# Attention of the first 768 tokens in tiles of four 32-query groups, ahead of two chained MLPs

## Chip, core and metric

One core of a Trainium2 chip. The metric is the device time of one launch in microseconds; for the kernel before it is 935.74 us, the median of three runs.

## What is computed

Four batches of 576 tokens with 8 heads of 64 channels go through an attention that adds two parts, and the 2304 x 512 result goes through two MLPs. All is float32 at the interface.

```python
# q, k, v: (4, 8, 576, 64); factor = 4; scale = 1 / 8
q_d, k_d, v_d = (x.reshape(B, H, 144, 4, D).mean(axis=3) for x in (q, k, v))
out_up = np.repeat(sm_attn(q_d, k_d, v_d), 4, axis=2)      # coarse attention over 144 averaged rows
mask = np.abs(pos[:, None] - pos[None, :]) < 4              # a band of 7 keys
out_local = softmax(where(mask, scale * q @ k.T, -1e9)) @ v
x = (out_up + out_local) as (2304, 512)
x = (s * relu(x @ w_in) ** 2 + b) @ w_out                   # d_ff 2048
x = ((x @ w_a) * (x @ w_b)) @ w_out2                        # d_ff 1536
```

## The kernel before

The program is written as a list of tasks (`Program.add`: an engine, a duration, what it reads, the buffers it takes and gives back, a due time), and `Program.order` plans it when the program is built: at each step it takes the task that could start first by its own model of times, and of equal ones the one that is due first. Each engine then runs its instructions in that order, so constants of the planner (`T0`, `DUE_*`, the durations, the numbers of buffers in `RAMP_BUFS`) move instructions on every engine.

There are three stages.

The **ramp** does the attention of tokens 0 to 767. `down` (L558) does the coarse attention of one pair of heads of one batch: keys and queries are loaded (L278) and added in fours (`prep`, on DVE at L582 for batch 0, on GpSimd at L584 and L585 for batch 1), then scores (L620), maxima (L634), exponentials (L647), normalisation (L662), transposes (L671) and the value product (L691). For batch 0 the pooled values are loaded in two halves of 72 rows per pair and summed by a reduction (L603); for batch 1 GpSimd's queue adds them up by transfers (L551). `tile_job` (L729) does the band of 7 keys for a tile of 96 tokens, all 8 heads: mask matmul (L774) and scores (L780) over 102 keys, maxima (L802), eight exponentials with an accumulator each (L816), normalisation of 816 elements (L831), eight transposes (L839), their copies (L849), the value product (L857), the sum with the coarse part (L871), and the split of the result into a high and a low part (`split_x`, L497 on ACT, L501 on DVE). There are eight such tiles, and a tile's 102 value rows come in one transfer. Between them PE runs matmuls on zeros (L273), whose number is planned, to keep busy.

The **first MLP** goes over six blocks of 384 tokens and 16 slices of d_ff each. A slice has 12 first-layer matmuls (L1059 to L1061, four groups of three) and 12 second-layer ones (L1102 to L1104), relu, square and copy on ACT (L1076 to L1083), and a subtraction on DVE (L1087). Block 0 needs its 32 weight slices decoded while it runs: each takes three ACT passes (L342, L349, L378) and three DVE passes (L354, L362, L383). The attention of the other 1536 tokens is done meanwhile, in `unit` on DVE. The **second MLP** (L1347 and L1487 to L1489) follows.

On SP all loads stand in one planned order, and POOL has its own. The change touches the ramp's tiles, loads and constants, and the planner.

```python
ts = add("PE", 1.75, s_fn, ..., [wide, wide, E_SLOT[ph]], ...,
    after=[mm["dS", b, hp] for hp in range(HP)], lead=LEAD, share=0.55)
```

This line of `tile_job` shows a task: a tile's scores come behind the coarse scores of its batch.

## Time and profile before

| | |
|---|---|
| runs | 934.76, 935.74, 935.96 us |
| span of the profiled execution | 932.3 us (its own time isn't given; the runs are 2.5 to 3.7 longer) |
| PE busy | 913.2 us, 98% |
| DVE busy | 789.9 us, 85% |
| ACT busy | 497.4 us, 53% |
| GpSimd busy | 69.7 us, 7% |
| first MLP matmul (L1059) | starts at 59.2 us |
| DMA, 0 to 60 us | 11.92 MB, 199 GB/s |
| DMA, 60 to 100 us | 296 GB/s, busy share 0.91 |

The shares are means over stages that differ: PE's 98% is full for most of the span, and its idle time is in the first 150 us. A busy time counts the overlap of neighbours, so the time from one start to the next is a little shorter than a duration. In the stretches, PEclk is the granted TensorE clock as a share of its full 2.4 GHz.

### The profile page before, as it was taken

Reading aid. Unit: us, or ns where it says so; the run is one execution under the profiler, and the core shown is the slowest. Engines: PE = TensorE matmul, PEld = TensorE weight load, DVE = VectorE, ACT = ScalarE, POOL = GpSimd, SP = SyncE. Lnnn points to the kernel's source line nnn. Section 1 sums busy time; section 2 is a strip of 40 time slices with the busy share of each in tenths; the row PEclk is TensorE's granted clock in tenths of the full one; section 3 lists DMA queues with packets and bytes.
Section 4 is the critical chain, followed back from the end, with each engine's and each line's share of the span. In section 5 each row is a group of like instructions: output and inputs, shape, how many; then the busy total and the mean of one; then the engine's idle time right before and its main releaser. Section 6 shows DMA issues by size and latency. Waiting matters only on the chain.

```text
span 932.3 us, 14367 instructions
## 1 busy us (share of the span) xinstructions
PE 913.2 (98%) x5319; PEld 847.0 (91%) x5319; DVE 789.9 (85%) x1388; ACT 497.4 (53%) x1144; POOL 69.7 (7%) x70
## 2 busy tenths in 40 slices
PE   8988999999999999999999999999999999999997
PEld 4667989998999899999999999999999999999996
DVE  6988998999999999995977999879877778877753
ACT  4989995345445443535988555335433336433322
POOL 2241201021322200000000000000000000000000
PEclk9998999999999999999999999999999999999999
DMA  7869626224354332313477342012200010300001
GB/s 206 241 174 332 156 90 194 82 82 133 115 115 114 103 107 69 102 29 136 148 262 261 122 122 82 23 44 81 102 22 3 24 43 13 102 29 18 1 1 69
DMA packets 46864, 96.76 MB, mean 104 GB/s; under 512 B 6393, under 2 KB 21337, under 8 KB 46409
## 3 DMA queue, kind: packets, MB, share of 16 engines
q1 hardware_dynamic: 39160, 92.77, 31.0%
q0 software_dynamic: 7200, 2.67, 2.5%
q8 instruction: 42, 0.69, 0.3%
q10 hardware_dynamic: 432, 0.39, 0.1%
q14 instruction: 30, 0.24, 0.1%
HBM read 83.22 MB, written 12.58 MB: 103 GB/s over the span
## 4 chain that ended last, share of the span: by engine, by line
PE 84%; DVE 5%; ACT 4%; issue 3%; DMA 2%; POOL 1%; SPq 0%; ACTq 0%
PE ab L1347 28%; PE acc L1102 7%; PE acc L1103 6%; PE h L1059 6%; PE acc L1104 6%; PE h L1061 6%; PE h L1060 6%; PE acc L1488 5%; PE acc L1489 5%; PE acc L1487 5%; DVE pr L969 1%; DMA pv<-in_vd_dram 1%; ACT z L342 1%; DMA tq<-in_bmask_dram 1%; ACT w L378 1%
## 5 line engine op out<-in xcount | busy, mean ns | idle before, releaser
L1347 PE MATMUL ab<-xo,w 128*128 128x384 f32 x1376 | 273.7, 338 | 0.4 <-DVE u L1390 0.4
L1347 PEld LDWEIGHTS ab<-xo,w 128*128 128x128 f32 x1376 | 246.1, 188 | 16.3 <-DVE u L1390 0.7
L1102 PE MATMUL acc<-gh,w 128*128 128x384 f32 (+1 forms) x384 | 134.2, 350 | 4.0 <-ACT w L816 2.0
L1103 PE MATMUL acc<-gl,w 128*128 128x384 f32 x384 | 131.2, 342 | 0.0
L1059 PE MATMUL h<-xsh,w 128*128 128x384 f32 x384 | 131.1, 341 | 0.0
L1104 PE MATMUL acc<-gh,w 128*128 128x384 f32 (+1 forms) x384 | 130.5, 340 | 0.0
L1061 PE MATMUL h<-xsh,w 128*128 128x384 f32 x384 | 129.0, 336 | 0.0
L1060 PE MATMUL h<-xsl,w 128*128 128x384 f32 x384 | 129.0, 336 | 0.0
L1076 ACT ACTIVATE u<-h 128x384 f32<-128x384 f32 x96 | 47.1, 491 | 116.3 <-PE h L1061 114.9
L1463 ACT ACTIVATE gh<-u 128x384 fp32r<-128x384 f32 x69 | 36.2, 524 | 84.6 <-DVE u L1424 50.5
L1102 PEld LDWEIGHTS acc<-gh,w 128*128 128x128 f32 x384 | 73.0, 190 | 8.1 <-ACT w L816 2.6
L1059 PEld LDWEIGHTS h<-xsh,w 128*128 128x128 f32 x384 | 72.2, 188 | 2.4 <-issue 2.0
L1103 PEld LDWEIGHTS acc<-gl,w 128*128 128x128 f32 x384 | 73.1, 190 | 0.9 <-DVE gl L1087 0.9
L1104 PEld LDWEIGHTS acc<-gh,w 128*128 128x128 f32 x384 | 73.0, 190 | 0.0
L1060 PEld LDWEIGHTS h<-xsl,w 128*128 128x128 f32 x384 | 72.2, 188 | 0.0
L1061 PEld LDWEIGHTS h<-xsh,w 128*128 128x128 f32 x384 | 72.1, 188 | 0.0
L1087 DVE TENSOR_TENSOR gl<-u,gh 128x384 fp32r<-128x384 f32 x96 | 54.3, 565 | 15.4 <-ACT gh L1083 15.2
L1371 ACT ACTIVATE w<-ab 128x384 f32<-128x384 f32 x31 | 15.2, 491 | 95.2 <-PE ab L1347 93.4
L1489 PE MATMUL acc<-w,gl 128*128 128x512 f32 x138 | 54.4, 394 | 0.0
L1488 PE MATMUL acc<-w,gh 128*128 128x512 f32 x138 | 54.3, 394 | 0.0
L1487 PE MATMUL acc<-w,gh 128*128 128x512 f32 x138 | 54.2, 393 | 0.0
L354 DVE TENSOR_SCALAR w<-w 128x512 uint16<-128x512 f32 x61 | 45.6, 767 | 8.3 <-ACT w L349 8.0
(207 smaller groups left out, 1743.9 us busy)
## 6 DMA issues: line engine op xcount, KB each, us to landing
w<-in_w_a_dram SPq DMA_DIRECT2D x26, 512.0 KB
w<-in_w_o_dram SPq DMA_DIRECT2D x25, 512.0 KB
bk<-in_ku_dram SPq DMA_DIRECT2D x22, 320.0 KB
bk<-in_vu_dram SPq DMA_DIRECT2D x22, 320.0 KB
w<-wod SPq DMA_DIRECT2D x12, 512.0 KB
w<-in_w_b_dram SPq DMA_DIRECT2D x10, 512.0 KB
x2d<-ev SPq DMA_DIRECT2D x24, 192.0 KB
x<-x2d SPq DMA_DIRECT2D x3, 1536.0 KB
```

The source lines that it names most:

```text
L1059: nc.tensor.matmul(out=st["h"], lhsT=w[:, 0, k], rhs=hi[:, k], start=(k == 0), stop=False)
L1060: nc.tensor.matmul(out=st["h"], lhsT=w[:, 0, k], rhs=lo[:, k], start=False, stop=False)
L1061: nc.tensor.matmul(out=st["h"], lhsT=w[:, 1, k], rhs=hi[:, k], start=False, stop=(k == HP - 1))
L1076: A_.activation(out=st["u"], in_=st["h"], func=ACTF.Relu)
L1087: V.tensor_tensor(out=st["lo"], in0=st["u"], in1=st["hi"][:, :n].bitcast(F32), op=ALU.subtract)
L1102: nc.tensor.matmul(out=acc, lhsT=wh, rhs=st["hi"], start=(f == 0), stop=False)
L1103: nc.tensor.matmul(out=acc[:, :n], lhsT=wh, rhs=st["lo"], start=False, stop=False)
L1104: nc.tensor.matmul(out=acc, lhsT=wl, rhs=st["hi"], start=False, stop=(f == FA - 1))
L1347: nc.tensor.matmul(out=o, lhsT=w[:, k], rhs=x, start=(not more and k + n == 0), stop=(k == 1 and n == 2), skip_group_check=more,)
L1487: nc.tensor.matmul(out=acc, lhsT=gh, rhs=w[:, 0], start=first, stop=False)
L1488: nc.tensor.matmul(out=acc, lhsT=gh, rhs=w[:, 1], start=False, stop=False)
L1489: nc.tensor.matmul(out=acc, lhsT=gl, rhs=w[:, 0], start=False, stop=last)
```

## The change

The ramp's 768 tokens are cut into six tiles of 128, and a tile into four groups of 32 queries, each with its own 38 keys. Scores of the four groups stand below one another in 128 partitions, so everything per tile runs over 8 x 38 = 304 elements in place of 816. The subtraction of the maximum is an instruction of its own on DVE (L872), the exponential is one ACT instruction (L882) with the sum as a DVE reduction (L888), and four transposes of 128 x 128 (L905) replace eight. In turn a tile has more matmuls: 32 for a tile's scores (L839) and 32 for its value product (L924), of 38 and 32 columns. Tile 4 spans two batches, so four tiles (not six) read batch 0's whole keys and queries. A tile's values come in four transfers, of 32 and 6 rows for each of two halves of the heads. Batch 0's pooled values come in one transfer per pair and are summed by two adds (L650, L651) in place of two reductions. The mask and the identity are cast on GpSimd, the ACT table is loaded at the start, and key and query sums have four buffers each. The planner now models 16 transfer engines and at most 8 transfers under way, need not put a dummy matmul between two tasks, and has other durations and due times.

```diff
-TQ = 96
+TQ = 32
+NQ = 4
+TT = NQ * TQ
-JOBS = ["TTTTTT", "TTUUU", "UUUUu", "uUUUU"]
+JOBS = ["G" * 18, "GGGGGGUUU", "UUUUu", "uUUUU"]
+PATIENCE = 0.15
-T0, STEP = 40.2, 4.018 / 384
+T0, STEP = 32.0, 4.018 / 384
-WARM, FILL_MIN, FILL_MAX = 18, 1, 20
+WARM, FILL_MIN, FILL_MAX = 18, 0, 20
-RAMP_BUFS = {"dq": 2, "dk": 2, "dv": 2, "qd": 1, "kd": 1, "vp": 4, "tq": 1, "tk": 1, "tv": 2, "e": 1, "x": 1, "z": 2}
+RAMP_BUFS = {"dq": 2, "dk": 2, "qd": 4, "kd": 4, "tq": 1, "tk": 1, "tv": 1, "e": 2, "x": 1, "z": 2}
+ISSUE, QUEUE, DMA_START, POOL_START, DMA_LAND = 0.46, 8, 1.0, 1.4, 0.95
...
+                    if e == "SP" and len(landed) >= QUEUE:
+                        s = max(s, landed[-QUEUE])
...
+def wires(rows, pieces, size, each=0.0):
+    n = max(i for i in range(1, 17) if rows % i == 0)
+    return n, rows // n * pieces * (each or 0.010 + size / 25e3)
...
+        A_.activation(out=warm, in_=ones, func=ACTF.Exp)
...
-                        V.tensor_reduce(out=d, in_=x.rearrange("p r c -> p c r"), axis=AX.X, op=ALU.add)
+                eng.tensor_tensor(out=x[:, :, 0:2], in0=x[:, :, 0:2], in1=x[:, :, 2:4], op=ALU.add)
+                eng.tensor_tensor(out=x[:, :, 0], in0=x[:, :, 0], in1=x[:, :, 1], op=ALU.add)
...
-        load(l_v, TW * DM * 4, writes=[("tv", i)], acq=[(names["tv"],)], after=after)
+        for u in range(2):
+            for a, r in ((0, 32), (32, TW - 32)):
...
+                for g in range(NQ):
+                    q, k, k0, k1 = qk(g, hp)
+                    nc.tensor.matmul(
+                        out=sc[h][g * TQ:g * TQ + TQ, hp, k0:k1], lhsT=q[h * D:h * D + D], rhs=k[h * D:h * D + D],
+                        start=False, stop=(hp == HP - 1),
+                    )
...
+                V.tensor_tensor(
+                    out=e[:, h, :, :, :TW], in0=st["sc"][h].rearrange("p (u m) k -> p u m k", u=2),
+                    in1=st["nb"][:, h].rearrange("p (u m) -> p u m", u=2).unsqueeze(3).to_broadcast([TT, 2, 2, TW]),
+                    op=ALU.subtract,
+                )
...
-                for hp in range(HP):
-                    j = h * HP + hp
-                    A_.activation(
-                        out=e[:, j], in_=st["sc"][h][:, hp], func=ACTF.Exp, scale=scale, bias=st["nb"][:, j:j + 1],
-                        accum_out=sm[:, j:j + 1],
-                    )
+            A_.activation(out=e_view(), in_=e_view(), func=ACTF.Exp, scale=scale)
...
+            V.tensor_reduce(out=sm, in_=e_view(), axis=AX.X, op=ALU.add)
```

How the order moves shows at three places. On DVE, one tile's softmax before, from its maxima to the scaling and to the next tile's maxima (`tnb` and `tsm` are maxima and sums, `vp` pooled values):

```order
L802 TENSOR_REDUCE tnb<-sc 96x4 x2
L824 TENSOR_SCALAR tsm<-tsm 96x8
L603 TENSOR_REDUCE vp<-dv 72x128
L827 RECIPROCAL tsm<-tsm 96x8
L805 TENSOR_SCALAR tnb<-tnb 96x8
L831 TENSOR_TENSOR w<-w,tsm 96x816
L603 TENSOR_REDUCE vp<-dv 72x128
L802 TENSOR_REDUCE tnb<-sc 96x4 x2
```

And the same place in the changed kernel, the first tile:

```order
L707 TENSOR_TENSOR w<-w,sm 72x576
L866 TENSOR_REDUCE tnb<-sc 128x4 x2
L872 TENSOR_TENSOR e<-sc,tnb 128x2x2x38 x2
L403 TENSOR_SCALAR w<-w 128x512
L888 TENSOR_REDUCE tsm<-e 128x8
L891 TENSOR_SCALAR tsm<-tsm 128x8
L894 RECIPROCAL tsm<-tsm 128x8
L898 TENSOR_TENSOR e<-e,tsm 128x8x38
L866 TENSOR_REDUCE tnb<-sc 128x4 x2
```

The pooled values no longer stand between the tiles' steps (they are ahead of the first tile), and the first weight step (L403) does.

On PE, the last instructions ahead of the first MLP matmul before, which come behind the value product of the sixth tile:

```order
L671 MATMUL at<-ident,w 72x72 x8
L273 LDWEIGHTS wz
L273 MATMUL pw<-wz 128x408
L857 MATMUL o<-w,tv 64x96 x8
L1059 MATMUL h<-xsh,w 128x384
L1060 MATMUL h<-xsl,w 128x384
L1061 MATMUL h<-xsh,w 128x384
```

And in the changed kernel, where the scores of tile 4 and the transposes of batch 1's last pair of heads are ahead of it:

```order
L839 MATMUL sc<-tk,tq 32x38
L716 MATMUL at<-ident,w 72x72 x8
L1131 MATMUL h<-xsh,w 128x384
L1132 MATMUL h<-xsl,w 128x384
L1133 MATMUL h<-xsh,w 128x384
```

All four coarse scores of batch 1 are now ahead of the first h matmul; before, the fourth came after two groups of it.

On GpSimd, the key and query sums of batch 1 (`kd`, `qd`) and the transfers that add up its values (`pv`) before:

```order
L551 DMA pv<-in_vd_dram 72x4x128
L584 ISA
L584 TENSOR_TENSOR dk<-dk 128x144x2
L585 TENSOR_TENSOR kd<-dk 128x144
L584 TENSOR_TENSOR dq<-dq 128x144x2
L585 TENSOR_TENSOR qd<-dq 128x144
L551 DMA pv<-in_vd_dram 72x4x128 x4
L584 TENSOR_TENSOR dk<-dk 128x144x2
L585 TENSOR_TENSOR kd<-dk 128x144
```

And in the changed kernel:

```order
L633 TENSOR_TENSOR dq<-dq 128x144x2
L634 TENSOR_TENSOR qd<-dq 128x144
L633 TENSOR_TENSOR dk<-dk 128x144x2
L634 TENSOR_TENSOR kd<-dk 128x144
L633 TENSOR_TENSOR dq<-dq 128x144x2
L634 TENSOR_TENSOR qd<-dq 128x144
L633 TENSOR_TENSOR dk<-dk 128x144x2
L634 TENSOR_TENSOR kd<-dk 128x144
L600 DMA pv<-in_vd_dram 72x4x128
```

The first five sums now stand ahead of the first of these transfers, where before four transfers stood between the first pair of heads and the second.

## Rows read from the trace of the kernel before

**Rows 1.** Stretches of the span: length, busy us (instructions) of PE, PEld, DVE, ACT, POOL; PEclk, DMA share, GB/s.
```profile
0.00:59.20 59.20, 50.64 (x467) 31.41 (x467) 47.81 (x109) 40.18 (x184) 21.20 (x26) 0.97 0.74 201
59.20:143.00 83.80, 79.68 (x508) 73.09 (x505) 76.59 (x149) 81.74 (x199) 9.02 (x7) 0.96 0.63 192
150.00:504.00 354.00, 353.58 (x2122) 343.70 (x2122) 322.10 (x475) 188.47 (x424) 39.49 (x38) 1.00 0.41 124
```
**Rows 2.** L1059 and L1102 until 143.5 us: count, ns min/median/max, first and last start.
```profile
L1059 PE MATMUL h<-xsh,w x64: 331/338/446, 59.2 to 143.2; 128*128 128x384 f32 x64
...
L1102 PE MATMUL acc<-gh,w x56: 333/342/671, 71.0 to 141.0; 128*128 128x386 f32 x56
```
**Rows 3.** Timeline of PE: start, us, what [idle before <- releaser].
```profile
77.25 0.44 PE L1102 MATMUL acc<-gh,w 128*128 128x386 f32 x1 [1.47 <-ACT w L816]
```
**Rows 4.** Timeline of DVE.
```profile
18.39 0.81 DVE L634 TENSOR_REDUCE nb<-sc 72x2 f32<-72x288 f32 x2
19.12 0.16 DVE L658 RECIPROCAL sm<-sm 72x4 f32<-72x4 f32 x1
...
20.20 0.74 DVE L662 TENSOR_TENSOR w<-w,sm 72x576 f32<-72x576 f32 x1
20.87 1.05 DVE L802 TENSOR_REDUCE tnb<-sc 96x4 f32<-96x408 f32 x2
...
28.12 1.00 DVE L831 TENSOR_TENSOR w<-w,tsm 96x816 f32<-96x816 f32 x1
29.04 1.03 DVE L603 TENSOR_REDUCE vp<-dv 72x128 f32<-72x512 f32 x1
...
43.28 1.61 DVE L831 TENSOR_TENSOR w<-w,tsm 96x816 f32<-96x816 f32 x1
...
62.71 0.68 DVE L362 SCALAR_TENSOR_TENSOR z<-z,w 128x512 int32<-128x512 int32 x1
63.31 0.74 DVE L354 TENSOR_SCALAR w<-w 128x512 uint16<-128x512 f32 x1
63.84 0.73 DVE L362 SCALAR_TENSOR_TENSOR z<-z,w 128x512 int32<-128x512 int32 x1
```
**Rows 5.** Groups of DVE, 0 to 60 us: busy us, mean ns | idle before, releasers.
```profile
L582 DVE TENSOR_REDUCE kd<-w 128x144 f32<-128x576 f32 x4 | 3.0, 747 | 5.6 <-PE sc L620 3.1 <-DMA w<-in_kT_dram 2.5
```
**Rows 6.** Groups of ACT, 0 to 150 us.
```profile
L816 ACT ACTIVATE w<-sc,tnb 96x102 f32<-96x102 f32 x48 | 15.7, 370 | 0.4 <-DVE tnb L805 0.4
```
**Rows 7.** Stretches, columns as in rows 1.
```profile
10.00:20.00 10.00, 7.99 (x72) 4.54 (x67) 8.78 (x23) 6.56 (x27) 3.91 (x6) 1.00 0.66 161
...
20.00:51.80 31.80, 28.94 (x321) 19.50 (x321) 30.89 (x69) 29.43 (x142) 10.70 (x11) 1.00 0.85 223
...
80.00:85.30 5.30, 5.28 (x21) 5.28 (x22) 5.26 (x10) 5.30 (x12) 0.32 (x1) 0.50 1.09 359
```
**Rows 8.** Groups of PE, 59.2 to 150 us (first row), and steps of its timeline.
```profile
L1102 PE MATMUL acc<-gh,w 128*128 128x386 f32 x63 | 23.4, 371 | 4.0 <-ACT w L816 2.0 <-DVE gh L1089 1.4 <-ACT u L1076 0.5
...
62.88 0.93 PE L780 MATMUL sc<-tk,tq 64*96 64x99 f32 x16
63.73 0.70 PE L671 MATMUL at<-ident,w 72*72 72x72 f32 x8
64.36 0.71 PE L691 MATMUL o<-w,pv 72*64 72x144 f32 x8
65.00 0.45 PE L1059 MATMUL h<-xsh,w 128*128 128x384 f32 x1
```
**Rows 9.** DVE's last xsl, and L1059 until 436 us.
```profile
428.46 0.69 DVE L501 TENSOR_TENSOR xsl<-x,xsh 128x512 fp32r<-128x512 f32 x1 [0.70 <-ACT xsh L497]
...
L1059 PE MATMUL h<-xsh,w x318: 331/336/446, 59.2 to 434.8; 128*128 128x384 f32 x159
```
**Rows 10.** Timeline of POOL.
```profile
18.00 0.44 POOL L585 TENSOR_TENSOR kd<-dk 128x144 f32<-128x144 f32 x1
...
51.15 1.94 POOL L585 TENSOR_TENSOR kd<-dk 128x144 f32<-128x144 f32 x1
```

More of the change, by code (lines that the diff above doesn't have):

```diff
@@ L41 @@
             UNITS.append((_t, 4 if _j == "U" else 2))
-        _t += {"T": TQ, "U": 128, "u": 64}[_j]
+        _t += {"G": TQ, "U": 128, "u": 64}[_j]
     assert _t == _b * S + S
+GROUPS = [list(range(i, i + NQ)) for i in range(0, len(TILES), NQ)]
+assert all(TILES[g[0]] == i * TT for i, g in enumerate(GROUPS)) and len(GROUPS) * TT == RAMP
 def _edge(t0, R):
```

367 lines of the change are left out of this document (206 added, 161 removed).

## Prediction

> **What bounds the kernel now.** Start with the stretches [rows 1]: from 150 to 504 us TensorE is busy 353.58 of 354.00 at full clock, so from there on the time is matmul work that the change leaves alone, and what can move is the moment at which that work gets going. Then look for that moment. The 64th L1059 matmul, the last first-layer group of block 0, starts at 143.2 with 56 groups of L1102 done [rows 2]; the order of the changed kernel has the same 64 and 56 ahead of that place. So I work out how much earlier the 64th comes and shift everything after it by that. The time up to it falls in two: 59.2 us until the first h matmul, and 84.0 us for the 64 groups. Until 59.2 DVE is busy 47.8, PE 50.6 (much of it dummies), ACT 40.2 [rows 1]: no engine is full, but DVE starts at 3.6 and has the longest work that must be done, so it sets the first part. In the second part ACT is busy 81.74 of 83.80 and DVE 76.59.
>
> **Until the first matmul.** I count DVE's instructions in the new order ahead of the xsl of the third tile (block 0 now needs three tiles of 128, not four of 96) and price them start to start [rows 4]. A pair of score maxima (L634) goes in 0.73; 576 elements (L662) in 0.67; 816 elements (L831) in 0.92; 512 elements of L362 in 0.60; L354 in 0.53; the tiny ones in 0.08. By these, about 1 ns an element and some 0.07 us each, 304 elements cost 0.38 and a pair of 152 costs 0.45.
> - 8 reductions of q and k at 0.67: 5.4; 8 pairs of maxima at 0.73: 5.8; 8 normalisations at 0.67: 5.4; 24 tiny ones: 2.0.
> - 4 value sums, now two adds of 512 and 256 elements (0.60 and 0.33): 3.7.
> - 4 tiles at two pairs of 152 (maximum, subtraction), two passes of 304 and 0.2 of tiny ones: 1.86 each, 7.4.
> - 15 weight steps (6 at 0.53, 9 at 0.60): 8.6. Three x and xsl at 0.67 and 0.60: 3.8.
>
> Sum 42.1. To this comes the start, 3.6, and the idle time. Before, DVE was idle 59.2 - 47.8 - 3.6 = 7.8 after its start; 3.1 of it was the second key sum waiting for a PE matmul to give back the one kd buffer [rows 5], and kd and qd now have four each, so that goes; the next late thing there is the landing of the keys, already in the 4.7 that I keep. GpSimd's key and query sums of batch 1 now run from about 20 (5.0 MB of loads are ahead of the first keys, at the rate worked out below) to 40 us beside DVE. One collision in rows 4 made L831 take 1.61 instead of 1.00. Bounds: none, and every one of its 16 instructions blocking DVE for some 0.55, which is 8.8. I take four such collisions, 2.4, since the rows show a few. That gives 3.6 + 42.1 + 4.7 + 2.4 = 52.8, and with tile 4's scores and one group of transposes, which PE has ahead of its first h matmul and which end about then, **53.5** (before 59.2).
>
> The other things ahead of it. ACT loses most: eight exponentials per tile at 0.37, each with an accumulator to read [rows 6], become one pass of 304 elements; that is slack here, since ACT is not what DVE waits for. The mask casts go from DVE to GpSimd, which is idle until the first keys of batch 1 land, and cost nothing; without that cover they would be half a microsecond on GpSimd. The table load moves into the first 2 us, where ACT has nothing else. The 8 value transfers of 102 rows and the 8 of pooled values become 24 parts of 32 and of 6 rows and 4 whole ones; SP issues more, but they are queued behind the same q and k loads and ahead of weights, in 10.1 MB (summed from the loads' sizes in the order) that must land before the last query pair of batch 1. At the best rate of the ramp, 223 GB/s at a share of 0.85 [rows 7], so 262 by estimate if the engines are full, that takes until 40; GpSimd, PE, DVE and ACT then need about 7 for that pair's softmax, so 47, which DVE's 53.5 hides. At 223 it is 54, at 201 (the mean until 59.2) 57.
>
> **From the first matmul to the 64th group.** 120 groups of three at 0.1745 are 62.8 of the 84.0. Of the rest PE waited 4.0 at L1102 [rows 8], 2.0 of it for L816, the exponentials, one wait of 1.47 of it at 77.25 [rows 3]; after it the clock was granted at 0.50 for 5.3 us [rows 7], 2.65 lost. L816 is gone, so 2.1 of waits go (what is late next is gh, which I leave in), and of the clock loss I take back 1.6. The rest of the attention: before, by counts times 80 ns (L691) and 54 ns (L780) a record and the transposes, 10.6. After, the order has four value products (2.6), two groups of transposes (1.0), one tile's masks (0.3), and three steps of 32 small matmuls, each two records as in rows 8: 64 records per step. Such a record of 32 to 38 columns has no row. From 54 ns at 102 columns and 80 at 144 it can't be above 54; by its columns it is 20. My estimate is 25, nearer the lower since the two rows follow the columns, so 1.6 a step and 8.7 in all, a saving of 1.9; the ends are 1.0 better and 5.6 worse. Sum: 84.0 - 2.1 - 1.6 - 1.9 = **78.4**.
>
> Can the weights keep up? DVE's whole list ahead of the last weight is, at the same prices, 104.7 (before 114.9). With 3.6, 4.7 and 2.4 it is done at 115, well before 53.5 + 78.4. ACT's list shrinks by more than 20. So PE is the limit there.
>
> **After that.** DVE's window attention feeds blocks 2 to 5. Its last xsl starts at 428.46 and 318 of the L1059 have started at 434.8 [rows 9]; the 321st, block 5's first, comes most of a slice later, at 438.4. The margin from the end of that xsl is 9.3. DVE has about 10 us less work ahead of it, so it moves by about as much as PE, and I leave the margin.
>
> **The sum.** 53.5 + 78.4 = 131.9 against 143.2: 11.3 less. The profiled span is 932.3 and the runs shown are 934.76 to 935.96, so some 3.4 lie around the span; the page gives no time of the profiled execution itself. I take the shift from the median: 935.74 - 11.3 = **924.4**.
>
> **Rivals.**
> - *The lock.* The value sums were reductions of one input; as adds they have two, and they now run at the very time at which GpSimd reads the keys. For: GpSimd's 0.44 became 1.94 beside DVE [rows 10]. Against: most of DVE's work there is reductions, and before only a few DVE instructions were stretched. If every GpSimd instruction blocks DVE, 8.8 instead of 2.4: first matmul at 59.9, end 930.8. Chance 0.10. The Trainium skill (SBUF — State Buffer, Who interferes with whom) states just this: a VectorE instruction with two SBUF inputs and a GpSimd instruction that reads SBUF exclude each other for a whole instruction, and a reduction never does. By that rule this rival's 930.8 is what the value sums' new form invites; the rows agree for the stretched pair and do not show that every one meets.
> - *The transfers.* At 201 GB/s the last queries land at 50, the first matmul starts at 57.3, and the end is 928.2. For: the engines were busy 0.85 at 223. Against: the value loads leave fewer engines idle. Chance 0.12.
> - *Slower.* The same place, SP's queue ahead of the last queries of batch 1, at the 161 GB/s of 10 to 20 us [rows 7], because the 6-row parts take a whole turn each: landing at 64, first matmul at 71, 149.4 against 143.2, so **941.9**. It turns slower where those queries land after 57.8, below about 178 GB/s. Chance 0.09. That the loads do not use 16 engines as the change says (72 rows and 6 rows don't divide by 16) would show here first.
> - *DVE with no idle time.* If 4.7 and 2.4 vanish, the first matmul comes at 47; with all waits and clock loss gone too the 64th group is at 122.4, DVE's weights still in time: 914.9. Chance 0.14.
> - *The margin in block 5.* If DVE's window work does not move with PE, 9.3 is all that can be won: 926.4. Chance 0.07.
>
> **How the numbers follow.** My forecast (924.4, within about 918 to 929) has 0.45. With 0.09 for slower and 0.03 for a first matmul near 64.8, which leaves the time the same, the other rivals hold the rest, all on the faster side. The range reaches to the lowest and the highest of the rivals that are faster, with the 5.6 of the small matmuls on top in part: 914 to 932. A measurement can tell 0.2%, 1.9 us, from no change. Faster 0.88, same 0.03, slower 0.09.
>
> **What would show it.** In the new profile: the first h matmul (L1131) near 53, the 64th near 132 with no wait of PE on an exponential; the granted clock at full from 55 on; DVE idle less than 8 us before the first matmul; the 32-column matmuls 25 ns apart; PE again full from 150 on. It is wrong if the first h matmul comes after 60, if DVE stops for batch 1's score maxima, or if PE gets waits on DVE between 200 and 440.

## The result and the profile after

The changed kernel takes 946.4 us (median of four runs, 943.0 to 949.4) against 935.85 for the one before, a ratio of 1.0117 with an interval of 1.0086 to 1.0148: **slower by 10.5 us**, where 924.4 was forecast. The profiled execution is of 948.74 us, span 946.7, so 14.4 longer than the profiled one before; one wait in it (at 77 us, below) does not fall in every execution of this order, as run 17 shows.

Four stretches of the changed kernel, cut at the first h matmul (L1131), the 64th and the 383rd; the columns are those of [rows 1]:

```profile
0.00:71.70 71.70, 54.44 (x877) 35.60 (x877) 49.55 (x127) 36.21 (x116) 21.25 (x30) 0.81 0.83 200
71.70:151.20 79.50, 78.01 (x592) 75.27 (x593) 66.37 (x134) 66.78 (x134) 8.14 (x7) 0.89 0.59 181
151.20:515.20 364.00, 362.12 (x2159) 349.46 (x2158) 328.51 (x485) 194.43 (x436) 37.27 (x38) 1.00 0.41 128
515.20:946.70 431.50, 424.56 (x2191) 393.47 (x2189) 338.44 (x646) 181.31 (x328) 0.00 (x0) 0.99 0.15 51
```

Before, the same four took 59.2, 84.0, 360.4 and 428.7 ([rows 1, 2]; the 383rd L1059 starts at 503.6). So the first h matmul comes 12.5 later, the 64th 8.0 later, the 383rd 11.6 later and the end 14.4 later: **8.0 are lost up to the 64th and 6.4 behind it**, 3.6 of these up to the 383rd and 2.8 after it.

Up to the first h matmul VectorE is busy 49.55 and idle 22, and the granted clock is 0.81 of full (0.97 in [rows 1]). TensorE's timeline shows where it stood, start, us, what, and in brackets the idle time before it and what ended it:

```profile
24.54 1.18 PE L716 MATMUL at<-ident,w 72*72 72x72 f32 x8 [3.48 <-ACT up L749]
...
43.53 1.49 PE L924 MATMUL o<-e,tv 38*64 38x32 f32 x56 [1.48 <-DMA tv<-in_tv_dram]
...
52.73 0.47 PE L839 MATMUL sc<-w 64*32 64x38 f32 x21 [3.29 <-issue]
...
57.89 1.30 PE L665 MATMUL sc<-kd,qd 64*72 64x144 f32 x8 [4.24 <-POOL qd L634]
...
71.75 0.66 PE L1131 MATMUL h<-xsh,w 128*128 128x384 f32 x1 [0.76 <-DVE x L941]
...
77.47 1.67 PE L737 MATMUL o<-w,pv 72*64 72x144 f32 x20 [1.44 <-DMA pv<-in_vd_dram]
```

The first: ScalarE stood 4.23 us for the transfer of the first weight, with three copies of attention queued behind that step. For the third ("issue") the profile names nothing; the last section says what it ends with. The second: the values of tile 0, whose four parts were issued over 26 us (SyncE's queue; `w<-in_tv` is the same transfer for tiles 1 to 3):

```profile
10.11 0.33 SPq L308 DMA_DIRECT2D tv<-in_tv_dram  x1
...
20.61 0.29 SPq L308 DMA_DIRECT2D tv<-in_tv_dram  x1
...
29.08 1.34 SPq L308 DMA_DIRECT2D tv<-in_tv_dram  x1
...
35.74 0.29 SPq L308 DMA_DIRECT2D tv<-in_tv_dram  x1
...
39.03 0.35 SPq L308 DMA_DIRECT2D dq<-in_qT_dram  x1
```

The plan lets a part be issued only when the part before it has landed by its reckoning, and fills the time with keys, queries and weights. The last row is the last query pair of batch 1, which the prediction took for the end of the queue that matters. Its sum came at 56.19, and not because of the load: in runs 1 and 2, where no accumulating transfer stands ahead of it, that load is issued at 40.25 and 38.45 and the sum, which waits for it, starts at 45.64 and 44.42. SyncE's and GpSimd's rows of run 2:

```profile
38.45 0.35 SPq L308 DMA_DIRECT2D dq<-in_qT_dram  x1
...
44.42 0.73 POOL L633 TENSOR_TENSOR dq<-dq 128x288 f32<-128x288 f32 x1 [3.91 <-DMA dq<-in_qT_dram]
```

GpSimd's timeline of the changed kernel:

```profile
35.68 1.33 POOL L600 DMA_DIRECT2D pv<-in_vd_dram  x1
...
45.54 1.22 POOL L600 DMA_DIRECT2D pv<-in_vd_dram  x1 [2.64 <-DMA w<-in_w_a_dram]
55.44 1.19 POOL L600 DMA_DIRECT2D pv<-in_vd_dram  x1 [8.68 <-issue]
56.19 1.14 POOL L633 TENSOR_TENSOR dq<-dq 128x288 f32<-128x288 f32 x1
57.40 0.43 POOL L634 TENSOR_TENSOR qd<-dq 128x144 f32<-128x144 f32 x1
61.34 1.58 POOL L600 DMA_DIRECT2D pv<-in_vd_dram  x1 [3.50 <-issue]
```

The accumulating transfers of batch 1's pooled values go one at a time, each 4 to 10 us after the one before (it is issued some 0.3 us after that one has landed), and what is queued behind one waits with it. Three stand ahead of the last query sum, two of them right before it. The last lands at 77.4, the wait ends at 77.47. Before the change they began 24 us sooner (SyncE's first plain one, GpSimd's first and last accumulating one):

```profile
5.98 0.38 SPq L549 DMA_DIRECT2D pv<-in_vd_dram  x1
...
12.01 1.32 POOL L551 DMA_DIRECT2D pv<-in_vd_dram  x1 [11.57 <-DMA pv<-in_vd_dram]
...
49.15 1.22 POOL L551 DMA_DIRECT2D pv<-in_vd_dram  x1 [1.89 <-DMA pv<-in_vd_dram]
```

Behind the wait at 77 the granted clock fell to 0.50, the 1.2 GHz level, and stayed there until about 92 (stretches of the changed kernel, TensorE alone; columns: length, PE busy, PEclk, DMA share, GB/s):

```profile
80.00:83.00 3.00, 3.00 (x14) 0.50 0.14 40
83.00:86.00 3.00, 3.00 (x68) 0.50 0.82 290
86.00:90.00 4.00, 4.00 (x75) 0.50 0.99 339
90.00:95.00 5.00, 5.00 (x25) 0.78 1.10 345
95.00:100.00 5.00, 5.00 (x87) 1.00 1.04 408
```

Behind the 64th one wait stands out, at the start of the second MLP (L1420 is L1347 before, which had 0.4 idle). Between the 64th and the 383rd none does: TensorE's waits there are 1.8 us in all (0.4 before, the longest 0.76), and the same matmuls follow one another a little slower (179 ns on average from an h matmul's start to the next start, 176.5 before). The costliest group behind the 383rd, with busy, mean ns and idle time:

```profile
L1420 PE MATMUL ab<-xo,w 128*128 128x384 f32 x1386 | 280.2, 339 | 1.9 <-DVE w L1484 1.8
```

### The profile page after: what moved, and what is told of

Read it like the earlier page. It is cut to its first block, busy times and chain, and to the rows that moved or that the text cites. A ratio compares the mean times of both kernels' runs of the same rounds, so it can differ in the third digit from the quotient of the medians.

```text
span 946.7 us, 15194 instructions
## 1 busy us (share of the span) xinstructions
PE 919.1 (97%) x5815; PEld 853.8 (90%) x5815; DVE 782.9 (83%) x1390; ACT 478.7 (51%) x1011; POOL 66.7 (7%) x74
## 4 chain that ended last, share of the span: by engine, by line
PE 72%; DVE 9%; DMA 7%; ACT 7%; issue 4%; SPq 1%; POOL 1%; DVEq 0%
PE ab L1420 28%; PE acc L1561 5%; PE acc L1562 5%; PE acc L1560 5%; PE acc L1174 4%; PE acc L1175 4%; PE h L1131 4%; PE acc L1176 4%; PE h L1133 4%; PE h L1132 4%; DMA tv<-in_tv_dram 2%; ACT w L398 1%; DVE pr L1041 1%; ACT z L391 1%; DVE gl L1159 1%
## 5 line engine op out<-in xcount | busy, mean ns | idle before, releaser
L1420 PE MATMUL ab<-xo,w 128*128 128x384 f32 x1386 | 280.2, 339 | 1.9 <-DVE w L1484 1.8
L1420 PEld LDWEIGHTS ab<-xo,w 128*128 128x128 f32 x1386 | 249.3, 189 | 18.7 <-DVE w L1484 2.8
L1131 PE MATMUL h<-xsh,w 128*128 128x384 f32 x384 | 133.0, 346 | 0.8 <-DVE x L941 0.8
L1133 PE MATMUL h<-xsh,w 128*128 128x384 f32 x384 | 130.4, 340 | 0.0
L1131 PEld LDWEIGHTS h<-xsh,w 128*128 128x128 f32 x384 | 73.4, 191 | 3.1 <-issue 2.1
L1175 PEld LDWEIGHTS acc<-gl,w 128*128 128x128 f32 x384 | 72.5, 189 | 2.5 <-DVE gl L1159 2.4
L1133 PEld LDWEIGHTS h<-xsh,w 128*128 128x128 f32 x384 | 73.3, 191 | 0.0
L1176 PEld LDWEIGHTS acc<-gh,w 128*128 128x128 f32 x384 | 72.5, 189 | 0.0
L1159 DVE TENSOR_TENSOR gl<-u,gh 128x384 fp32r<-128x384 f32 x96 | 54.1, 564 | 16.2 <-ACT gh L1155 16.2
L1444 ACT ACTIVATE w<-ab 128x384 f32<-128x384 f32 x33 | 16.2, 490 | 97.6 <-PE ab L1420 91.7
L1562 PE MATMUL acc<-wx,gl 128*128 128x512 f32 x150 | 59.1, 394 | 0.0
L1561 PE MATMUL acc<-wx,gh 128*128 128x512 f32 x150 | 59.0, 393 | 0.0
L1560 PE MATMUL acc<-wx,gh 128*128 128x512 f32 x150 | 58.9, 393 | 0.0
L403 DVE TENSOR_SCALAR w<-w 128x512 uint16<-128x512 f32 x62 | 45.7, 762 | 9.8 <-ACT w L398 9.6
```

The costliest lines, as they stand in the source:

```text
L1131: nc.tensor.matmul(out=st["h"], lhsT=w[:, 0, k], rhs=hi[:, k], start=(k == 0), stop=False)
L1133: nc.tensor.matmul(out=st["h"], lhsT=w[:, 1, k], rhs=hi[:, k], start=False, stop=(k == HP - 1))
L1159: V.tensor_tensor(out=st["lo"], in0=st["u"], in1=st["hi"][:, :n].bitcast(F32), op=ALU.subtract)
L1175: nc.tensor.matmul(out=acc[:, :n], lhsT=wh, rhs=st["lo"], start=False, stop=False)
L1176: nc.tensor.matmul(out=acc, lhsT=wl, rhs=st["hi"], start=False, stop=(f == FA - 1))
L1420: nc.tensor.matmul(out=o, lhsT=w[:, k], rhs=x, start=(not more and k + n == 0), stop=(k == 1 and n == 2), skip_group_check=more,)
```

## The experiments

Eighteen kernels ran. The changed kernel is the base unless another is named. Times are medians of the runs, the kernel before being 934.2 to 936.0 beside them; starts are of the profiled execution. The changed kernel's own runs spread by 6.3 us, so a gain of 2 or 3 on it is not clear of noise by its time alone. A dummy is one of the matmuls on zeros.

| edit | first h | 64th h | 64th to end | time |
|---|---|---|---|---|
| kernel before | 59.2 | 143.2 | 789.1 | 935.8 |
| changed kernel | 71.7 | 151.2 | 795.5 | 946.4 |
| 1 accumulating transfers behind the sums | 68.3 | 153.4 | 797.2 | 952.2 |
| 2 without them | 69.0 | 140.9 | 797.1 | 939.0 |
| 3 first weight step later | 72.2 | 144.2 | 795.8 | 942.9 |
| 4 = 2 and 3 | 68.0 | 139.9 | 795.4 | 937.4 |
| 5 values' parts unchained | 55.5 | 144.6 | 798.5 | 944.0 |
| 6 pooled values early | 78.0 | 147.0 | 797.1 | 952.0 |
| 7 = 5 and 6 | 56.3 | 140.4 | 799.6 | 941.8 |
| 8 planned with 15 GB/s | 72.3 | 156.5 | 788.0 | 947.4 |
| 9 = 2 and 5 | 57.2 | 134.6 | 798.2 | 933.7 |
| 10 pooled values added on GpSimd | 73.3 | 145.5 | 797.4 | 942.0 |
| 11 = 5 and 10 | 57.2 | 134.1 | 797.0 | 935.5 |
| 12 = 11, planned with 18 GB/s | 53.8 | 139.8 | 794.2 | 935.9 |
| 13 = 11 and twelve dummies | 55.8 | 133.8 | 798.3 | 937.2 |
| 14 = 11, values in 38 rows | 76.0 | 156.8 | 799.6 | 958.0 |
| 15 = 11, weights held | 51.8 | 135.2 | 796.8 | 933.0 |
| 16 a dummy everywhere | 72.5 | 145.2 | 796.4 | 943.7 |
| 17 planned with 15 behind 150 us | 74.2 | 146.9 | 790.3 | 939.0 |
| 18 = 15 and 17, dummies at two waits | 53.1 | 135.5 | 790.0 | 927.0 |

### 1 to 4: the waits one by one

The first theory, Q, took the waits above as separate faults of place; its rival, T, had all transfers late, so that another wait stands behind each. In the first, tasks of a finished plan are moved on GpSimd's queue alone (`late` are batch 1's accumulating transfers, `i` the last query sum's place):

```diff
+        L = [x for x in L[:i + 1] if x[0] not in late] + [x for x in L[:i + 1] if x[0] in late] + L[i + 1:]
```

> The changed kernel with one edit: on GpSimd's queue the three accumulating value transfers of batch 1 that stood ahead of the last query sum (one ahead of the third query sum, two ahead of the fourth) stand behind it; every other queue is untouched. Theory Q (the late first h is made by steps that stand in the wrong place on in-order queues): the 4.24 us that TensorE stood for that sum at 57.9 us goes, the last scores of batch 1 start near 53, the first h near 66 to 68 instead of 71.75, the run ends near 941 to 943 against 946.4. Theory T (nearly all transfers of the first 60 us land later than the plan has them, so that behind each wait stands another): the first h moves by under 1.5 us. Rival for both: the six transfers one behind another now end later, the products of batch 1 wait for them at 75 to 85 us, and the run is no faster than 946 whatever the first h does.

```diff
-                    else:
+                    elif b > 1:
                         G.dma_start(out=pooled[b][:, kh], in_=src[:, kh, :, r], accum_op=ALU.add)
```

> The changed kernel without the six accumulating value transfers of batch 1 (its pooled values are then those of every fourth row alone; this leaves that part of the sum out): nothing on GpSimd ahead of the last query sum but sums, and no product waits for a value transfer. Theory Q: as with the transfers moved, 4.2 us and the 1.4 us wait of the products, the first h near 65 to 67, the run near 939 to 942. Theory T: under 2 us, the run at 944 to 947, with the idle time of TensorE ahead of the first h put down to transfers, weights or instruction fetch.

In the third, ScalarE's first step of the first weight (`early[0]`) and the VectorE step behind it are moved to its second step:

```diff
+        early = [P.made["low", 0][0], P.made["sg", 0][0]]
+        a = [x for x in L[:i] if x[0] in early]
+        L = [x for x in L[:i] if x[0] not in early] + a[:1] + [L[i]] + a[1:] + L[i + 1:]
```

> The changed kernel with one edit: ScalarE's first step of the first weight (which stood 4.23 us for its transfer at 19 to 23 us, with three copies of attention behind it) and VectorE's step that reads it stand three copies later, ahead of the second step of the same weight. Theory Q: TensorE's 3.48 us idle at 21 to 24.5 us goes, and with it the fall of its granted clock (0.70 in 20 to 30 us), so that the transposes and products of 24.5 to 33.7 take 0.7 us a group and not 1.2: the batch-1 scores at 32.5 us come by 25 to 28, the first h by 3.5 to 7 us sooner, the run near 940 to 943. Theory T: the keys and queries of batch 1 are not there before 24 to 40 us anyway, the first h moves by under 1.5 us, and the run stays at 945 to 947.

> Both: no accumulating transfers of batch 1 (that part of the sum is left out) and ScalarE's first weight step three copies later. Theory Q: the two gains add, the first h near 58 to 63, the run near 933 to 939, that is about the time of the kernel before. Theory T: they do not add; the first h stays above 67 and the run above 942, and the rest of the loss lies in transfers (values of the third tile, instruction fetch) and in the clock.

Measured: 952.2, 939.0, 942.9 and 937.4. The first h matmul stayed at 68.0 to 72.2 in all four. In 3 and 4 that is T's; in 1 and 2 it moved by 3.4 and 2.7, between the two theories. The times of 2, 3 and 4 are those that Q gave, but not by its way: they moved by what lies behind the first h matmul. Run 1 is slower, as its rival for both said. From the first h matmul to the 64th it is 72.0, 71.9 and 71.9 us where no product waits for pooled values, 79.5 in the changed kernel, and 85.1 with the transfers moved back, where products waited 5.6 for them. The same matmuls without the wait, in run 2, which leaves the transfers out (columns as above):

```profile
74.00:77.50 3.50, 3.50 (x56) 1.00 0.14 36
77.50:80.00 2.50, 2.50 (x120) 1.00 0.98 354
80.00:83.00 3.00, 3.00 (x19) 1.00 0.95 269
```

So a wait of 1.44 us cost 7.6: the rest is the clock behind it. It explains part of 3 as well, which has no wait for pooled values either, though its edit is elsewhere. Run 17, whose order on TensorE is the changed kernel's up to there, has none: the same order meets this wait in one execution and not in another.

### 5 to 8: what sets the first h matmul

Theory V: the four parts of a tile's values, one behind another's landing. Theory P: the pooled values' place. Theory R: the plan's rate of 25 GB/s for an engine. The edit of the fifth is one rule of the plan:

```diff
-                u.ready = max(u.ready, t.end + (0.0 if u.eng == t.eng == "PE" else t.seen))
+                u.ready = max(u.ready, t.start + ISSUE if u.eng == t.eng == "SP" else t.end + (0.0 if u.eng == t.eng == "PE" else t.seen))
```

> The changed kernel with one rule of its plan altered: a transfer that follows another one on SyncE's queue may be issued right behind it, where the plan made it wait until the first had landed. It bears on the four value transfers of each tile (32, 6, 32 and 6 rows): they now stand together, tile by tile, ahead of the keys of batch 1; before, the four of tile 0 were issued at 10.1, 20.6, 29.1 and 35.7 us and the last landed at 43.4. Theory V (the values' pieces, one landing behind another, hold the tiles, and the batch-1 work was put ahead of them for that): the tile products come by 28 to 36 instead of 41.8 to 47 and 66 to 68, the first h at 56 to 63, the run at 930 to 938. Rival T (all transfers share 160 to 270 GB/s until 58 us whatever their order): now the keys of batch 1 and the first weights land later by what the values gain, the first h stays at 68 or later, and the run at 942 to 950.

```diff
-    pool_in(1, P.made["open", "r"], target(FA) - DUE_NEXT[0])
+    pool_in(1, P.made["open", "r"], target(FA) - DUE_NEXT[0] - 30)
```

> The changed kernel with the pooled values of batch 1 due 30 us earlier in the plan: their two plain transfers are issued among the first value transfers (before: 27.9 and 34.5 us; in the kernel before the change 6.0 and 18.8), and four of the six accumulating ones stand ahead of the second and third query sums on GpSimd. Theory P (the change put the pooled values' transfers 22 us later, and what it costs is TensorE's wait for the last at 77.4 us and the low granted clock of 77 to 92 us behind that wait): no wait for them, 72 us and not 79.5 from the first h matmul to the 64th, the run at 936 to 941, as with those transfers left out. Rival: each holds GpSimd 5 to 10 us, the key and query sums of batch 1 come later, the first h at 75 us or later, and what the clock gives back is lost there: 944 to 950.

> Both of these edits: values of a tile issued together, pooled values of batch 1 early. Theories V and P together: first h at 54 to 62, no wait for pooled values, 72 to 76 us from there to the 64th h matmul, the run at 924 to 934, below the kernel before. Rival T: first h at 66 or later, 938 to 948.

```diff
-    return n, rows // n * pieces * (each or 0.010 + size / 25e3)
+    return n, rows // n * pieces * (each or 0.010 + size / 15e3)
```

> The changed kernel, planned with 15 GB/s for each transfer engine instead of 25 (16 of them 240 GB/s and not 400; the trace of the changed kernel has 161 to 271 GB/s from 10 to 58 us at a busy share of 0.9 to 1.07). Only the order on the queues changes. Theory R (the order was made for transfers that land at 34 where they land at 45, so that TensorE's queue stands behind late ones): TensorE waits under 8 us in 20 to 70 where it waited 16, its clock stays above 0.85, the first h at 62 to 67, the run at 934 to 941. Rival V (not the rate but the four value transfers of a tile in a chain hold the first h): the plan knows the delay and still cannot avoid it, the first h stays at 67 to 72, and the run at 941 to 948.

V is right on the first h matmul, and neither other edit brought it forward: 55.5 instead of 71.7, since tile 0's products came at 27.5. Part of that is order: two of batch 1's four coarse softmaxes and seven of the 15 weight steps are no longer ahead of the third tile on VectorE. SyncE's queue in that run:

```profile
9.35 2.09 SPq L308 DMA_DIRECT2D tv<-in_tv_dram  x4
12.15 9.12 SPq L308 DMA_DIRECT2D w<-in_tv_dram  x12
```

But the time fell by 2.4 only, into the range of rival T (942 to 950). The accumulating transfers took over (TensorE's timeline of the same run):

```profile
66.41 0.47 PE L737 MATMUL o<-w,pv 72*64 72x144 f32 x4 [2.29 <-DMA pv<-in_vd_dram]
...
70.70 1.71 PE L737 MATMUL o<-w,pv 72*64 72x144 f32 x12 [3.83 <-DMA pv<-in_vd_dram]
```

Put early, they hold the sums of batch 1 instead: its first query sum came at 47.0 with TensorE waiting. TensorE's timeline of run 7:

```profile
47.50 1.24 PE L665 MATMUL sc<-kd,qd 64*72 64x144 f32 x8 [12.76 <-POOL qd L634]
```

So P's rival was right (run 6: 78.0 and 952.0): of the three places tried for six of them in a row, on the queue that also makes the sums, each costs. And R failed as put, as its rival said: planned with 15 GB/s throughout, the kernel takes 947.4, its first h matmul stays at 72.3 and the 64th comes at 156.5. But behind the 64th it needs 788.0, not 795.5.

### 9 to 12: both faults mended

Theory GV: the chain and, behind it, the accumulating transfers; W: weights set the 64th anyway. The mended kernel with a whole result loads batch 1's values whole and adds rows on GpSimd, as batch 0's on VectorE (`pool_in(1, ...)` goes):

```diff
-        if b == 0:
+        if b < 2:
             def lv(p):
...
-            name, eng, cost = ENG.get(V_ENG[hp], ("", None, None))
+            name, eng, cost = ENG.get(V_ENG[hp] if b == 0 else 'G', ("", None, None))
```

> The changed kernel with the value transfers of a tile issued one behind another (as in the run with that edit alone) and without the six accumulating transfers of batch 1 (this leaves that part of the pooled values out). With the values' edit alone the first h came at 55.5 us instead of 71.75, but the 64th only at 144.6: TensorE then stood 6.1 us for pooled values, and its granted clock was low in 30 to 40 and 70 to 80 us. Theory GV (two faults one behind the other: the values' chain sets the first h, and behind it the accumulating transfers, one landing after another at 4 to 10 us each, set the products of batch 1): first h at 53 to 56, the 64th at 126 to 132, the run at 922 to 930. Rival W (the weights' transfers and VectorE's list for 64 h groups set the 64th): 64th at 138 or later, the run at 936 to 943.

> The changed kernel with the pooled values of batch 1 made as those of batch 0 are: four whole transfers of 288 KB and GpSimd's additions of rows of four (8 instructions) in place of two plain and six accumulating transfers; the result is whole. The values of the tiles stay in their chain. Theory GV: the second fault alone is mended, as with the transfers left out: first h at 68 to 72, no wait for pooled values, 72 to 74 us to the 64th, the run at 937 to 942. Rival: 1.2 MB more at 230 GB/s (5 us) come ahead of tiles and weights, and the run stays at 945 to 950.

> Both faults mended with a whole result: pooled values of batch 1 added on GpSimd, value transfers of a tile one behind another. Theory GV: first h at 53 to 58, 64th at 128 to 136, the run at 924 to 932, below the kernel before (935.2). Rival W: 64th at 138 or later, 936 to 943.

> The same, planned with 18 GB/s for each transfer engine (288 GB/s) instead of 25. If what is left is the gap between planned and real landing, TensorE's waits ahead of the 64th h matmul are fewer by 3 to 8 us than in the run with 25, and the run is faster by 2 to 6 us; if what is left is a list of work or bytes, there is no difference over 1.5 us; as planning with 15 alone made nothing faster (947.4 against 946.4), a loss of up to 3 us is the rival's outcome.

933.7, 942.0, 935.5 and 935.9. Alone the second repair gives 4.4, the first 2.4; together they give 10.9 (946.4 to 935.5, a ratio to the kernel before of 1.0008, 0.9986 to 1.003). By the 64th h matmul of the profiled executions it is 5.7 and 6.6 alone and 17.1 together, where 7.6 of each is the wait at 77 that the changed kernel met. So one hides behind the other. In run 11 it comes at 134.1, 9.1 earlier than in the kernel before and inside GV's 128 to 136; in run 9 at 134.6, outside GV's 126 to 132 and short of W's 138. Both times are above GV's ranges (933.7 and 935.5), because 797.0 to 798.2 stay behind the 64th. The other rate, 18, gave the same time: the first h matmul 3.4 sooner, the 64th 5.7 later, 2.9 less behind it.

### 13 to 16: the clock, the split, the weights

```diff
+            k = P.made["to", 0][0] is t
+            keep_warm(t.fill + 12 * k)
```

> The kernel with both faults mended (pooled values of batch 1 added on GpSimd, a tile's value transfers one behind another) with one edit: twelve more dummy matmuls ahead of the products of the first tile, where TensorE stood 2.19 us (26.7 to 28.9 us), after which the granted clock was 0.50 in 30 to 40. Theory C (what is left ahead of the first h is the clock: the same groups took 2.51 and not 1.45 us for a tile's products, 1.24 and not 0.71 for scores, 0.34 and not 0.17 for a dummy): clock above 0.85 in 30 to 50, first h at 50 to 54 instead of 57.2, the run at 929 to 933 against 935.5. Rival: the twelve only stand in the way, or the next wait lets the clock fall a few us later: first h at 56 to 58, the run at 934 to 937.

The clock did rise, from 0.50 to 0.77. A stretch of run 11, columns of [rows 1]:

```profile
30.00:40.00 10.00, 9.97 (x243) 7.53 (x241) 7.98 (x23) 5.94 (x17) 4.41 (x7) 0.50 1.06 277
```

The same stretch of run 13:

```profile
30.00:40.00 10.00, 8.34 (x222) 5.97 (x223) 8.02 (x24) 5.88 (x16) 4.97 (x7) 0.77 1.06 286
```

The first h matmul came 1.4 sooner, the 64th 0.3, the time not at all (937.2). So the rival holds: the half of this fall of the clock that the dummies mended was worth nothing. That the clock costs nothing ahead of the first h matmul is not shown, since it stayed below full.

The next undoes the split of the values, with the order still planned for it. The 32-row transfer carries all 38 rows, the 6-row one is not issued:

```diff
-                    return st["v"][u * 64 + a:u * 64 + a + r], tv[j0:j0 + NQ, a:a + r, u * HP * D:(u + 1) * HP * D].rearrange(
+                    return st["v"][u * 64:u * 64 + TW], tv[j0:j0 + NQ, :, u * HP * D:(u + 1) * HP * D].rearrange(
...
+            if rows != 6:
                 nc.sync.dma_start(out=dst, in_=src)
```

> The kernel with both faults mended, with one edit: each half of a tile's values in one transfer of 38 rows in place of 32 and 6, at the place of the 32-row one. Theory E (the split is there to spread rows over the transfer engines: 38 rows go over 2 of them, 32 over 16): a transfer takes 4 to 8 times as long, 152 KB over two engines at 10 to 17 GB/s each is 4.5 to 7.6 us and eight of them come one behind another on the same two, so that TensorE waits for values ahead of the first products (28.9 us), the first h at 65 or later and the run over 942. Rival N (rows and pieces go over all engines anyway): fewer transfers to issue, first h at 55 to 58, the run at 933 to 937.

Theory E, and by far: 958.0, with the first products 19 us later than in run 11. A stretch of it (columns of [rows 1]):

```profile
20.00:30.00 10.00, 5.91 (x147) 4.24 (x140) 4.38 (x15) 2.22 (x7) 0.00 (x0) 1.00 0.14 48
```

The products wait 22.0 us there, but not for their own values: by the landings in the trace tile 0's two transfers are in at 22.6. They wait for ScalarE's copy of the transposed weights, which stands behind the first weight step, and that one waits for a transfer that SyncE issues only behind the values of tiles 1 to 3. SyncE's queue, then ScalarE's, in that run:

```profile
11.90 22.07 SPq L309 DMA_DIRECT2D w<-in_tv_dram  x6
34.01 3.04 SPq L309 DMA_DIRECT2D w<-in_w_a_dram  x1
...
46.02 0.65 ACT L399 ACTIVATE w<-w 128x512 int32<-128x512 uint16 x1 [22.50 <-DMA w<-in_w_a_dram]
...
47.31 0.59 ACT L915 ACTIVATE e<-at 102x512 f32<-102x512 f32 x1
```

So theory E is right on the number of engines and on the time, and not on what TensorE waits for: six transfers of 38 rows held SyncE's queue for 22.07 us, where run 5's twelve of 32 and 6 rows took 9.12. In the stretch from 20 to 30 us the transfer engines are busy for 0.14, 2.2 of the 16, and move 48 GB/s, 21 each. The Trainium skill (DMA: Bandwidth & Descriptors, Why a DMA increments its semaphore by 16 and not by 1) says that such a transfer runs on the largest number of engines, up to 16, that divides the slowest dimension on both sides, for 38 rows 2; the row of that stretch agrees. The split that the change makes is worth 22.5 us in an order planned for it.

```diff
+    for k in range(2, n_a):
+        for l in P.made["st", k]:
+            for d in P.made[("dq", (1, HP - 1))]:
+                l.deps.append(d)
+                d.succ.append(l)
```

> The kernel with both faults mended, with the weights from the third on not loaded before the last query transfer of batch 1 is in. Theory T (bytes: 10 to 58 us run at 160 to 310 GB/s with the transfer engines at 0.8 to 1.07 busy, and weights are in the way of keys, values and instruction fetch): first h at 50 to 54, no wait put down to issue, the run at 929 to 933. Rival W (then the weights come late for the h groups): TensorE waits on ScalarE's and VectorE's weight steps between 55 and 100, the 64th h no earlier than 134, the run at 935 to 941.

933.0, with the first h matmul at 51.8 and the 64th at 135.2: T's first h, W's 64th. Three kernels (11, 13 and 15) with first h matmuls 5.4 us apart have nearly the same 64th, 133.8 to 135.2: by these an earlier first h matmul alone wins nothing.

```diff
-            keep_warm(t.fill)
+            keep_warm(max(t.fill, int(t.eng == "PE" and t.start < 50)))
```

> The changed kernel itself with one dummy matmul more ahead of each of the 21 steps of TensorE before the first h that had none in the plan (the kernel before had at least one everywhere); nothing else moves. Theory C (the clock alone makes a good part of the loss): granted clock 0.9 or more in 20 to 60 us instead of 0.50 to 0.79, the first h at 66 to 69, the run at 940 to 944. Rival: the waits are 3 to 4 us long and single dummies do not bridge them; the clock falls as before, and the 21 of them cost 0.17 to 0.35 us each: the first h at 72 to 75, the run at 946 to 952.

943.7, which is in C's range, but with the clock still 0.50 in 50 to 60 us and the first h matmul at 72.5, as the rival has it. From there to the 64th 72.7, without the wait for pooled values. That is within the changed kernel's own runs: no verdict on the clock.

### 17 and 18: behind the 64th, and all together

```diff
-                    wire[j] = max(wire[j], first) + took
+                    wire[j] = max(wire[j], first) + took * (25 / 15 if s > 150 else 1)
```

> The changed kernel, planned with 15 GB/s for each transfer engine (not 25) for transfers that the plan starts behind 150 us; the order up to there is that of the changed kernel. Between the 383rd h matmul and the end the changed kernel takes 431.5 us where the one before takes 428.7, with a wait of 1.8 us for VectorE's weight step at the start of the second layer; planned with 15 throughout (947.4) that stretch took 427.3 with no such wait. Theory R2 (the cheap transfers of the plan cost that much there): no wait of 1.8 us, 427 to 429 us for that stretch, the run at 942 to 944. Rival: the difference came with the other constants of the change, the stretch stays at 431, the run at 945 to 948.

939.0. The wait for L1484 is gone, TensorE is full from 500 to 600 us, and the stretch behind the 383rd takes 427.2 instead of 431.5. Run 17, columns of [rows 1]:

```profile
500.00:600.00 100.00, 100.00 (x535) 94.88 (x534) 93.30 (x174) 62.83 (x114) 0.00 (x0) 1.00 0.36 124
```

The changed kernel in the first 60 us of this stretch:

```profile
500.00:520.00 20.00, 19.85 (x112) 19.26 (x111) 16.73 (x26) 18.51 (x37) 0.00 (x0) 1.00 0.78 282
520.00:560.00 40.00, 38.14 (x196) 35.67 (x195) 34.46 (x65) 19.09 (x35) 0.00 (x0) 0.96 0.32 108
```

R2 is right, and the time is below its 942 to 944. The two profiled executions differ by 9.5 in span: 5.2 behind the 64th, most of it behind the 383rd, and 4.3 up to the 64th, where this one lacks the wait at 77. Between the 64th and the 383rd it still takes 363.2 (360.4 before the change); no run was made for that alone. In the table all kernels planned with 25 need 795.4 to 799.6 behind the 64th, those planned with 15 there 788.0 to 790.3, the kernel before 789.1. Why the cheap transfers cost just that was not traced further than to L1484.

> What the runs so far found, together and with a whole result: pooled values of batch 1 added on GpSimd, a tile's value transfers one behind another, weights from the third on behind the last query transfer, 15 GB/s in the plan behind 150 us, and nine dummy matmuls more ahead of the products of the first and the fourth tile, where TensorE waited 1.6 and 1.8 us. If the late order gives 3 us and the clock behind those two waits (0.68 in 30 to 40, 0.54 to 0.66 in 50 to 70 us) is worth anything: 64th h matmul at 128 to 132 instead of 135.2, the run at 924 to 929, faster than the kernel before (935). If only the late order counts: 929 to 931. Rival: other waits take their place, 932 to 936.

**927.0** (924.3 to 927.4; ratio to the kernel before 0.9912, 0.9896 to 0.9929): faster than both kernels, with a whole result. The stretches, cut as at the top:

```profile
0.00:53.10 53.10, 44.20 (x787) 28.86 (x787) 42.10 (x105) 26.15 (x88) 22.01 (x32) 0.96 0.86 240
53.10:135.50 82.40, 77.56 (x674) 73.28 (x673) 75.43 (x156) 75.48 (x162) 8.72 (x6) 0.94 0.62 195
135.50:498.10 362.60, 360.38 (x2159) 349.68 (x2159) 323.67 (x476) 189.49 (x428) 42.58 (x38) 1.00 0.39 120
498.10:925.50 427.40, 422.43 (x2191) 392.25 (x2190) 342.90 (x655) 186.25 (x336) 0.00 (x0) 1.00 0.17 58
```

Against the one before, 7.7 are won up to the 64th, 2.2 given back to the 383rd, 1.3 won behind it. The dummies were worth nothing: the 64th stayed at 135.5. The gain on kernel 15, 6.0, lies behind the 64th (796.8 to 790.0), as the order behind 150 us would have it.

## Why the prediction was wrong, point by point

- *Until the first matmul* (53.5; measured 71.7): the step that failed. It took VectorE's list as the limit and kept 4.7 us of idle time; from its first reduction to the xsl of the third tile VectorE was idle 18. The list was too short as well: the same 120 instructions took 48.0 where 42.1 and 2.4 for collisions were reckoned, the tiny ones and the weight steps above all. The mended kernels' first h matmuls at 51.8 to 57.2 look like the forecast's 53.5 partly by luck, since their order has seven to eleven fewer weight steps and two fewer coarse softmaxes ahead of that xsl.
- *The other things ahead of it.* The sentence that went wrong is that the parts of the values are "queued behind the same q and k loads and ahead of weights". Of tile 0's four parts only the first is; the last was issued at 35.74, behind three weights. I summed bytes up to the last queries and never asked when a tile's values are whole. Unchaining them brings the first h matmul 11.8 to 16.2 us forward (69.0 to 57.2, 73.3 to 57.2, 71.7 to 55.5) and the 64th 6.3 to 11.4. The bytes themselves were priced nearly right: the last queries were in at about 45 by runs 1 and 2, where the forecast had 40 at best and 50 at 201 GB/s.
- *The step left out.* GpSimd's order was on record with the accumulating transfers moved behind the sums, and I priced the sums only. In the trace before, each starts 5.7 to 10.4 us before the next; at that, six in a row from 35.68 are not done before about 70. Leaving them out gives 7.4 alone and 10.3 with the values unchained (944.0 to 933.7).
- *A term put at nothing.* TensorE has 877 matmuls up to its first h matmul where it had 467. I priced their time and not their fetching: TensorE waited 4.1 us for instructions there (last section).
- *From the first matmul to the 64th* (78.4; measured 79.5): right by accident. Where no product waits, it is 71.9 to 72.7, and the loss of clock that I had taken back (1.6) came back as one of 6 behind another wait. Beyond the groups (62.8) and the attention (8.7) the forecast kept 6.9 from the kernel before, for which 71.9 leaves 0.4 at those prices; that is most of what was too dear. The small matmuls, estimated at 25 ns a record, take 11 to 12 in a tile's scores and 22 to 23 in its product at full clock, up to 0.9 us less a step.
- *Weights*: right; no wait of TensorE on a weight ahead of the 64th in the changed kernel.
- *After that*: wrong by 6.4. That TensorE's work behind the 64th moves as a block is right for block 5, where no wait for xsl appears. But I took the planner's new cost of transfers for a matter of the ramp, and it orders the whole program: 5.2 to 7.5 us behind the 64th by runs 17 and 8.
- *The sum.* With values and pooled values mended the 64th is at 134.1, where 131.9 was forecast, and with the late order as well 927.0 stands against 924.4. So about this shift can be had, from an order that differs from the changed kernel's in more than the two faults, and by other terms: 53.1 and 82.4 in run 18, not 53.5 and 78.4.
- *The rivals.* The slower one gave nearly the numbers (first h 71, 64th 149.4, 941.9), by another mechanism: the last queries were issued at 39.03, and what their sum waited for stood on GpSimd's queue, not on SyncE's. Its sentence on 6-row parts was near, but it is their chain, not their turn on the engines: 38-row transfers are worse. The lock: the value sums ran from 13.77 to 21.4, when GpSimd had no sum, and took 0.66 and 0.34 start to start, about as reckoned. VectorE's L891 took 1.25 at 56.11, beside GpSimd's sum at 56.19, where the shortest took 0.16; VectorE was not the limit there, so nothing followed. The margin in block 5 appears in no run. Nine of the eighteen wait for an xsl at the start of block 2 instead, 1.5 to 1.7 us at 209 to 233 us, whether their 64th is early or late; the changed kernel does not.
- *What would show it.* Two of the three signs against me came: the first h matmul after 60, and VectorE stopping for batch 1's maxima (1.80 us at 59.16, behind L665). Of the third, TensorE waiting for VectorE between 200 and 440, there is 0.69 us at 218.6 (0.19 at 213.3 before). TensorE had no wait on ScalarE's exponentials, as forecast. Clock full from 55: no.

The chance of 0.09 for slower was too small for a change that reorders every queue: the forecast priced instructions and took the order's waits as given.

## What to carry to other kernels

Where a load is cut into parts, ask of the new order when the *last* part is issued, and what was put between: bytes ahead of one named load do not tell it. List what stands on each in-order queue ahead of the item that others wait for, GpSimd's transfers and ScalarE's steps that wait for a load too, and give each the time to the next from the rows, not the time that the plan has. A wait's source is the end of such a chain: run 14's looked like values and was a weight. A cost model changed for one stage reorders all of them, so compare every stage's length, not only the one that the change is about.

## What the hardware showed unexpectedly

- A wait of 1.44 us of TensorE was followed by 15 us at the 1.2 GHz level, though TensorE was busy all through: 7.6 us in all.
- Transfer engines that show as full moved 175 GB/s from 10 to 20 us and 408 from 95 to 100 in the same run (11 and 25 GB/s each). The size of the pieces is not all of it: in the first stretch, value loads and the first weight above all, two thirds of the bytes go in pieces of 4 KB, as nearly all do in the second, and by the trace such a piece took 369 ns on average in the first and 164 in the second. Why is open. Two engines with 38-row value transfers and little beside them made 21 each.
- In rows of 64 small matmuls TensorE stood 0.4 to 5.1 us with nothing in the profile that it waited for ("issue"), mostly between 42 and 75 us, in the changed kernel and in all but run 15 of the eighteen, and not before the change, whose rows have 16. The trace's transfers settle what it waited for. The queue that the profile calls "instruction" brings 45 packets of 16 KB for the 11,715 matmuls and weight loads of the changed kernel, one for about 260. Of the 35 such waits of 0.4 us or more in these nineteen kernels, rows of other matmuls included, 34 end 1.2 to 1.8 us after one of these packets has ended (52.73 behind 51.18 in the changed kernel). By this it is its instructions that TensorE waits for. What makes a packet late is not shown: early weights held back go with short waits (none of 0.4 in run 15, 0.8 in run 18), but run 7, where they were not, has only one of 0.46.
